# RWKV attention into a squared-ReLU FFN on one core: the opening rearranged, with weights loaded and cast by GpSimd DMAs

## The chip, the core and the metric

The kernel runs on one core of a Trainium2 chip. A core has five engines that run side by side and wait for one another through semaphores: TensorE (PE) multiplies matrices into PSUM, VectorE (DVE), ScalarE (ACT) and GpSimd (POOL) work elementwise, and SyncE (SP) issues DMAs. The metric is the time of one execution on the device, in microseconds (us). The kernel before took 206.65 us, the median of three runs from 206.44 to 207.22. The profile is of one execution, whose span from the first to the last instruction is 203.6 us.

## What is computed

The reference is a linear attention with decay, for batch 4, 8 heads, 768 positions and head size 48, and then an FFN over the 3072 tokens:

```python
def _attn_ref(r, k, v, w, u):
    state = zeros((B, H, D, D))
    for t in range(S):
        kt, vt, rt = k[:, :, t], v[:, :, t], r[:, :, t]
        cur = einsum('bhd,bhe->bhde', u[None] * kt, vt)
        y[:, :, t] = einsum('bhd,bhde->bhe', rt, state + cur)
        state = w[None, :, :, None] * state + einsum('bhd,bhe->bhde', kt, vt)
    return y
# x = y as (3072 tokens, 384)
h = maximum(x @ w_in, 0)          # w_in  384 x 2048
out = (h * h) @ w_out             # w_out 2048 x 384
```

The kernel splits the 768 positions into six chunks of 128, so there are 24 chunks (six for each of four batches), numbered so that chunks 0 to 3 are the first chunk of each batch. Inside a chunk the recurrence becomes masked matrix products, and a state per batch carries over to the next chunk. Two chunks form a group of 256 tokens; there are 12 groups.

## The kernel before

The pools, the loads and the casts. Weights arrive in float32 in sixteen slices and GpSimd casts each to bfloat16:

```python
loads = ctx.enter_context(tc.tile_pool(name="loads", bufs=7))
psA: 1 bank   psY: 1 bank   psU: 1 bank   psH: 2 banks   psO: 2 banks     # PSUM, abridged
...
def load(i):                       # r, k, v of chunk i, 192 KB each
    nc.sync.dma_start(out=rf, in_=r_v[b, c])
    nc.sync.dma_start(out=kf, in_=k_v[b, c])
    nc.sync.dma_start(out=vf, in_=v_v[b, c])
def load_w1(s):                    # load_w2 alike
    t = stage.tile([128, CCH, GT], FP32, name=f"W1f_{s}", tag="W1f", bufs=NS)
    nc.sync.dma_start(out=t, in_=w_in_t[:, :, GT * s : GT * (s + 1)])
def cast_w1(s):                    # cast_w2 alike
    t = const.tile([128, CCH, GT], BF16, name=f"W1_{s}")
    nc.gpsimd.tensor_copy(t, W1f[s])
```

The parts of a chunk: `prep` scales k and r by decays, `prep_du` and `bonus` make the term with u, `turn` transposes, `piece_A` makes the masked scores, `piece_YU` the output and the state's update, `piece_X` the transposed input of the FFN:

```python
def prep(i, eng):
    eng.tensor_mul(rk_buf[i % NB][:, 1, :, 0:D], kf, Wkhat)
    eng.tensor_mul(rk_buf[i % NB][:, 0, :, 0:D], rf, Wt2)
def prep_du(i, eng):
    eng.tensor_mul(P0, rf, kf)
    eng.tensor_mul(P0, P0, ub)
def turn(i):
    if i < 4:      # on TensorE, through a psH bank, copied out by nc.scalar.copy(rkT, pt)
    else:          # nc.sync.dma_start_transpose(rkT, src)
def piece_A(i):
    # 8 products rkT x rkT -> Ap (psA)
    for e in range(2):
        nc.vector.tensor_mul(Bm[:, e], Ap[:, e], mask_b)
def piece_YU(i):
    # products -> Y (psY) and, unless it is a batch's last chunk, U (psU)
    nc.vector.tensor_add(xs, Y, dv)
    if c < NCH - 1:
        if c == 0:
            nc.vector.tensor_mul(S0W[b], U, WLm)
        else:
            nc.vector.tensor_add(ts, U, S0W[b])
            nc.gpsimd.tensor_mul(S0W[b], ts, WLm)
def piece_X(i):
    # 3 transposes of xs -> px (psU)
    nc.scalar.copy(xTs[g][:, :, L * j : L * (j + 1)], px)
```

The FFN goes in eight pieces per group: `piece_F1` makes 256 hidden features, `piece_F2` a quarter of the output of one chunk:

```python
def piece_F1(g, s):
    hp = psH.tile([128, 2, GT], FP32, name=f"hp_{g}_{s}", tag="H")
    # 6 products W1[s] x xT -> hp
    nc.scalar.activation(hr, hp, AF.Relu)
    if s % 4 == 3:
        nc.scalar.activation(hq, hr, AF.Square)
    else:
        nc.vector.tensor_mul(hq, hp, hr)
def piece_F2(g, s):
    j, q = s // 4, s % 4               # chunk of the group, quarter of the features
    # 4 products hq x W2 -> o (psO); after q == 3: nc.scalar.copy(osb, o), DMA to out
```

The order. In a period of the steady part, step s runs FFN1 of one group, FFN2 of the group before, and attention of the group after:

```python
def att(g, s):      # a, b = 2 * g, 2 * g + 1
    s == 0: cast_v(a); piece_A(a); bonus(a)
    s == 2: cast_v(b); piece_A(b); bonus(b)
    s == 3: piece_YU(a)    s == 4: piece_YU(b)    s == 5: piece_X(a)    s == 6: piece_X(b)
def preps(g, s):    # for the next group, on GpSimd
    s == 0: prep(2g); turn(2g)          s == 2: prep_du(2g)
    s == 4: prep(2g+1); turn(2g+1)      s == 6: prep_du(2g+1)
...
for i in range(4):
    prep(i, nc.vector)
    prep_du(i, nc.gpsimd)
    turn(i)
    if i % 2 == 1:
        period(i // 2, None, None)     # attention of groups 0 and 1
for s in range(NS): cast_w1(s)
for s in range(NS): cast_w2(s)
for i in (4, 5):
    prep(i, nc.gpsimd); turn(i); prep_du(i, nc.gpsimd)
load(6); load(7)
period(None, 0, None)                  # FFN1 of group 0
period(None, 1, None)                  # FFN1 of group 1
period(2, None, 0)                     # attention of group 2, FFN2 of group 0
for g in range(2, NG + 1):
    period(g + 1 if g + 1 < NG else None, g if g < NG else None, g - 1)
```

Of the kernel before, what the change touches and what calls it, by code (L numbers as in the profile page):

```python
# [16 lines left out]
def kernel(  # L17
# [29 lines left out]
    const = ctx.enter_context(tc.tile_pool(name="const", bufs=1))  # L47
    stage = ctx.enter_context(tc.tile_pool(name="stage", bufs=3))
    loads = ctx.enter_context(tc.tile_pool(name="loads", bufs=7))
    work = ctx.enter_context(tc.tile_pool(name="work", bufs=3))  # L50
# [34 lines left out]

    W1f, W2f, W1, W2 = [], [], [], []

    def load_w1(s):
        t = stage.tile([128, CCH, GT], FP32, name=f"W1f_{s}", tag="W1f", bufs=NS)
        nc.sync.dma_start(out=t, in_=w_in_t[:, :, GT * s : GT * (s + 1)])  # L90
        W1f.append(t)

    def load_w2(s):
        t = stage.tile([128, 2, d_model], FP32, name=f"W2f_{s}", tag="W2f", bufs=NS)
        nc.sync.dma_start(out=t, in_=w_out_t[:, 2 * s : 2 * s + 2, :])
        W2f.append(t)

    def cast_w1(s):
        t = const.tile([128, CCH, GT], BF16, name=f"W1_{s}")
        nc.gpsimd.tensor_copy(t, W1f[s])  # L100
        W1.append(t)

    def cast_w2(s):
        t = const.tile([128, 2, d_model], BF16, name=f"W2_{s}")
        nc.gpsimd.tensor_copy(t, W2f[s])
        W2.append(t)
# [8 lines left out]
    for i in range(1, 4):  # L115
        load(i)
    for s in range(NS):
        load_w1(s)
    for s in range(NS):
        load_w2(s)  # L120
        if s == 3:
            load(4)
    load(5)

# [30 lines left out]
    for j in range(NB):  # L155
        t = const.tile([128, 2, H, DP], BF16, name=f"rk_{j}")
        nc.vector.memset(t[:, :, :, D:DP], 0.0)
        rk_buf.append(t)
    wrow = const.tile([1, 2, HP, 128], FP32, name="wrow")
    nc.vector.memset(wrow, 0.0)  # L160
    esel = const.tile([1, 2, 2 * D], FP32, name="esel")
    nc.vector.memset(esel, 0.0)
    nc.vector.memset(esel[:, 0, 0:D], 1.0)
    nc.vector.memset(esel[:, 1, D : 2 * D], 1.0)

# [5 lines left out]
    nc.scalar.activation(Wt2, logw, AF.Exp, scale=tcol)  # L171
    logw_p = logw.rearrange("p (a e) d -> p e a d", e=2)
    for e in range(2):
        nc.scalar.activation(  # L174
            wrow[:, e, :, 64 * e : 64 * e + D], logw_p[0:1, e], AF.Exp, scale=float(L)
        )

    WLm = const.tile([128, HP, 2 * D], FP32, name="WLm")
    wl_ps = psU.tile([128, HP, 2 * D], FP32, name="wl_ps", tag="U", padded_shape=[None, None, 128])
    for hc in range(HP):  # L180
        for e in range(2):
            nc.tensor.matmul(  # L182
                wl_ps[:, hc, :],
                wrow[:, e, hc, :],
                esel[:, e, :],
                start=(e == 0),
                stop=(e == 1),
                skip_group_check=True,
            )
    nc.scalar.copy(WLm, wl_ps)  # L190

# [33 lines left out]
    def turn(i):  # L225
        rkT = work.tile([128, 2, HP, 128], BF16, name=f"rkT_{i}", tag="rkT", bufs=4)
        rkTs[i] = rkT
        src = rk_buf[i % NB]
        if i < 4:
            pt = psH.tile([128, 2, HP, 128], BF16, name=f"pt_{i}", tag="H")  # L230
            for j in (1, 0):
                for hc in range(HP):
                    nc.tensor.transpose(
                        pt[:, j, hc, :],
                        src[:, j, 2 * hc : 2 * hc + 2, :].rearrange("p a b -> p (a b)"),
                        identity,
                    )
            nc.scalar.copy(rkT, pt)
        else:
            nc.sync.dma_start_transpose(  # L240
                rkT.rearrange("p j a t -> p (j a) t"), src.rearrange("p j h d -> p (j h d)")
            )

    def piece_A(i):
# [16 lines left out]
        Bms[i] = Bm  # L261

    def piece_YU(i):
        c, b = i // B, i % B
# [26 lines left out]
        xss[i] = xs  # L291
        if c < NCH - 1:
            if c == 0:
                nc.vector.tensor_mul(S0W[b], U, WLm)
            else:
                ts = work.tile([128, HP, 2 * D], FP32, name=f"ts_{i}", tag="ts")
                nc.vector.tensor_add(ts, U, S0W[b])
                nc.gpsimd.tensor_mul(S0W[b], ts, WLm)  # L298
# [15 lines left out]
    def piece_F1(g, s):  # L314
        xT = xTs[g]
        hp = psH.tile([128, 2, GT], FP32, name=f"hp_{g}_{s}", tag="H")
        for fi in range(2):
            for c in range(CCH):
                nc.tensor.matmul(  # L319
                    hp[:, fi, :],  # L320
                    W1[s][:, c, 128 * fi : 128 * (fi + 1)],
                    xT[:, c, :],
# [6 lines left out]
        hq = hid.tile([128, 2, GT], BF16, name=f"hq_{g}_{s}", tag=f"hq{s}")  # L329
        if s % 4 == 3:  # L330
            nc.scalar.activation(hq, hr, AF.Square)
        else:
            nc.vector.tensor_mul(hq, hp, hr)
# [4 lines left out]
    def piece_F2(g, s):  # L338
        j, q = s // 4, s % 4
        i = 2 * g + j  # L340
        if q == 0:
            ops[i] = psO.tile([128, d_model], FP32, name=f"o_{i}", tag="O", padded_shape=[None, 512])
        for f in range(4 * q, 4 * q + 4):
            nc.tensor.matmul(
                ops[i],
                hsq[g, f // 2][:, f % 2, L * j : L * (j + 1)],
                W2[f // 2][:, f % 2, :],
                start=(f == 0),
# [9 lines left out]
    def att(g, s):  # L358
        a = 2 * g
        b = a + 1  # L360
        if s == 0:
            cast_v(a)
            piece_A(a)
            bonus(a)
        elif s == 2:
            cast_v(b)
            piece_A(b)
            bonus(b)
        elif s == 3:
            piece_YU(a)  # L370
# [7 lines left out]
    def preps(g, s):  # L378
        if g >= NG:
            return  # L380
        if s == 0:
            prep(2 * g, nc.gpsimd)
            turn(2 * g)
        elif s == 2:
            prep_du(2 * g, nc.gpsimd)
        elif s == 4:
            prep(2 * g + 1, nc.gpsimd)
            turn(2 * g + 1)
        elif s == 6:
            prep_du(2 * g + 1, nc.gpsimd)  # L390

    def period(ga, g1, g2):
        for s in range(8):
            if g1 is not None:
                piece_F1(g1, s)
            if g2 is not None:
                piece_F2(g2, s)
            if ga is not None:
                att(ga, s)
                if ga > 1:  # L400
                    preps(ga + 1, s)
                if s == 7 and ga > 1:
                    load(2 * ga + 4)
                    load(2 * ga + 5)

    for i in range(4):
        prep(i, nc.vector)
        prep_du(i, nc.gpsimd)
        turn(i)
        if i % 2 == 1:  # L410
            period(i // 2, None, None)
    for s in range(NS):
        cast_w1(s)
    for s in range(NS):
        cast_w2(s)
    for i in (4, 5):
        prep(i, nc.gpsimd)
        turn(i)
        prep_du(i, nc.gpsimd)
    load(6)  # L420
    load(7)
    period(None, 0, None)
    period(None, 1, None)
    period(2, None, 0)
    for g in range(2, NG + 1):
        period(g + 1 if g + 1 < NG else None, g if g < NG else None, g - 1)

# [29 lines left out]
```

## Time and profile before

| | busy us | share of the 203.6 us span |
|---|---|---|
| TensorE (PE) | 168.7 | 83% |
| VectorE (DVE) | 133.2 | 65% |
| GpSimd (POOL) | 117.8 | 58% |
| ScalarE (ACT) | 109.9 | 54% |
| DMA queue of SyncE | 30.81 MB | 66.3% of 16 engines |

The granted clock of TensorE is 0.999 of full over the span. A line of the timeline gives the start and the duration in us, the engine, the line of the kernel, the operation, the tile written and the tiles read (buffer numbers as the program gives them), their shapes and, in brackets, how long the engine stood idle before it and what ended that. A row of the windows view gives a stretch of time, its length, the busy time of PE, of PE's weight loads, of DVE, ACT and POOL with the number of instructions, the granted clock, the busy share of the DMA engines and what they moved in GB/s.

### The profile page before, as it was taken

The page shows a single profiled execution, that of the slowest core. Times are in us where ns is not written, and L with a number is a line of the kernel's source. Part 1 is how long each engine was busy: PE and PEld are TensorE (multiplying, and loading weights), DVE is VectorE, ACT ScalarE, POOL GpSimd, SP SyncE. Part 2 cuts the span into 40 slices and gives each one's busy share as a digit, 9 for nine tenths or more (in the row PEclk, how much of TensorE's full clock was granted, in tenths as well). Part 3 has the DMA queues.
Part 4 walks back from the last instruction along what each step waited for, and adds up shares of the span by engine and source line. Part 5 has one row for each costly group of instructions (what it writes and reads, how often), then busy time and mean ns, then how long its engine had stood idle before and what let it go on. Part 6 is the DMA issues. An engine that isn't in the chain of part 4 may idle for free.

```text
span 203.6 us, 4241 instructions
## 1 busy us (share of the span) xinstructions
PE 168.7 (83%) x1624; PEld 123.2 (61%) x1624; DVE 133.2 (65%) x230; ACT 109.9 (54%) x203; POOL 117.8 (58%) x130
## 2 busy tenths in 40 slices
PE   0763647677959998998999989989989899999992
PEld 0643434455546776775767757767767577677761
DVE  4379793454966939849759489397595783963310
ACT  3360613657516484575574745755756657556640
POOL 2487973891856494692992965938929749100000
PEclk9999999999999999999999999999999999999999
DMA  5999999829714946929929649689499396311112
GB/s 109 208 209 279 384 351 252 223 52 192 146 40 94 207 118 142 197 77 194 219 54 210 152 109 214 96 176 207 60 210 180 92 210 120 84 42 39 39 40 79
DMA packets 105140, 31.07 MB, mean 153 GB/s; under 512 B 96672, under 2 KB 105120, under 8 KB 105120
## 3 DMA queue, kind: packets, MB, share of 16 engines
q1 hardware_dynamic: 105120, 30.81, 66.3%
q8 instruction: 12, 0.20, 0.4%
q14 instruction: 8, 0.07, 0.1%
HBM read 20.84 MB, written 4.72 MB: 126 GB/s over the span
## 4 chain that ended last, share of the span: by engine, by line
PE 25%; POOL 24%; DVE 20%; DMA 13%; SPq 8%; issue 5%; ACT 4%; ACTq 0%
SPq L83 2%; SPq L81 2%; DMA kf_1562<-in_k_dram 2%; DMA kf_2056<-in_k_dram 2%; DMA kf_1315<-in_k_dram 2%; DMA kf_1809<-in_k_dram 2%; DMA kf_1068<-in_k_dram 2%; DMA rf_110<-in_r_dram 2%; DMA vf_828<-in_v_dram 2%; POOL rk_180 L199 1%; POOL rk_178 L199 1%; POOL rk_182 L200 1%; POOL rk_178 L200 1%; POOL S0W_211 L298 1%; POOL rk_182 L199 1%
## 5 line engine op out<-in xcount | busy, mean ns | idle before, releaser
L319 PEld LDWEIGHTS <-W_0_439 128*128 128x128 bf16 x72 | 7.3, 102 | 3.0 <-issue 0.9
L319 PEld LDWEIGHTS <-W_2_443 128*128 128x128 bf16 x72 | 7.1, 99 | 3.3 <-issue 1.3
L182 PE MATMUL wl_ps<-esel,wrow 1*128 1x96 f32 x16 | 3.7, 423 | 6.5 <-ACT wrow L174 6.5
L319 PEld LDWEIGHTS <-W_6_451 128*128 128x128 bf16 x72 | 6.6, 97 | 2.6 <-issue 1.9
L319 PEld LDWEIGHTS <-W_3_445 128*128 128x128 bf16 x72 | 6.4, 97 | 2.9 <-issue 1.2
L319 PEld LDWEIGHTS <-W_4_447 128*128 128x128 bf16 x72 | 6.5, 97 | 2.4 <-issue 1.7
L319 PEld LDWEIGHTS <-W_1_441 128*128 128x128 bf16 x72 | 6.6, 102 | 2.0
L182 PEld LDWEIGHTS wl_ps<-esel,wrow 1*128 1x128 f32 x16 | 3.5, 325 | 6.5 <-ACT wrow L174 6.5
L319 PEld LDWEIGHTS <-W_7_453 128*128 128x128 bf16 x72 | 6.7, 98 | 0.7
L319 PEld LDWEIGHTS <-W_5_449 128*128 128x128 bf16 x72 | 6.5, 98 | 0.7
L199 POOL TENSOR_TENSOR rk_180<-kf_486,Wkhat 128x384 bf16<-128x384 f32 x1 | 1.0, 1007 | 4.9 <-DMA kf_486<-in_k_dram 4.9
L309 ACT COPY xT_315<-px_316 128x384 bf16<-128x384 bf16 x1 | 0.5, 479 | 6.2 <-PE px_316 L308 6.2
L309 ACT COPY xT_428<-px_429 128x384 bf16<-128x384 bf16 x1 | 0.5, 479 | 6.0 <-PE px_429 L308 6.0
L205 POOL TENSOR_TENSOR P_0_215<-rf_90,kf_91 128x384 f32<-128x384 f32 x1 | 1.4, 1366 | 4.0 <-DMA kf_91<-in_k_dram 4.0
L199 POOL TENSOR_TENSOR rk_176<-kf_821,Wkhat 128x384 bf16<-128x384 f32 x1 | 1.0, 998 | 4.6 <-DMA kf_821<-in_k_dram 4.6
L199 POOL TENSOR_TENSOR rk_180<-kf_1068,Wkhat 128x384 bf16<-128x384 f32 x1 | 1.0, 999 | 4.1 <-DMA kf_1068<-in_k_dram 4.1
L199 POOL TENSOR_TENSOR rk_180<-kf_1562,Wkhat 128x384 bf16<-128x384 f32 x1 | 1.0, 1007 | 4.0 <-DMA kf_1562<-in_k_dram 4.0
L199 POOL TENSOR_TENSOR rk_180<-kf_2550,Wkhat 128x384 bf16<-128x384 f32 x1 | 1.0, 1000 | 4.1 <-DMA kf_2550<-in_k_dram 4.1
L199 POOL TENSOR_TENSOR rk_180<-kf_2056,Wkhat 128x384 bf16<-128x384 f32 x1 | 1.0, 1002 | 4.0 <-DMA kf_2056<-in_k_dram 4.0
L199 POOL TENSOR_TENSOR rk_176<-kf_2303,Wkhat 128x384 bf16<-128x384 f32 x1 | 1.0, 1006 | 3.9 <-DMA kf_2303<-in_k_dram 3.9
L199 POOL TENSOR_TENSOR rk_176<-kf_1315,Wkhat 128x384 bf16<-128x384 f32 x1 | 1.0, 997 | 3.9 <-DMA kf_1315<-in_k_dram 3.9
L199 POOL TENSOR_TENSOR rk_176<-kf_1809,Wkhat 128x384 bf16<-128x384 f32 x1 | 1.0, 1004 | 3.8 <-DMA kf_1809<-in_k_dram 3.8
(1126 smaller groups left out, 669.7 us busy)
## 6 DMA issues: line engine op xcount, KB each, us to landing
W1f_116<-in_moe_w_in_dram SPq DMA_DIRECT2D x1, 384.0 KB, 4.8
W1f_118<-in_moe_w_in_dram SPq DMA_DIRECT2D x1, 384.0 KB, 5.1
W1f_120<-in_moe_w_in_dram SPq DMA_DIRECT2D x1, 384.0 KB, 5.8
W1f_122<-in_moe_w_in_dram SPq DMA_DIRECT2D x1, 384.0 KB, 6.2
W1f_124<-in_moe_w_in_dram SPq DMA_DIRECT2D x1, 384.0 KB, 6.8
W1f_126<-in_moe_w_in_dram SPq DMA_DIRECT2D x1, 384.0 KB, 6.6
W1f_128<-in_moe_w_in_dram SPq DMA_DIRECT2D x1, 384.0 KB, 6.8
W1f_130<-in_moe_w_in_dram SPq DMA_DIRECT2D x1, 384.0 KB, 6.7
```

What stands on the lines that cost most here:

```text
L81: nc.sync.dma_start(out=rf, in_=r_v[b, c])
L83: nc.sync.dma_start(out=vf, in_=v_v[b, c])
L182: nc.tensor.matmul(wl_ps[:, hc, :], wrow[:, e, hc, :], esel[:, e, :], start=(e == 0), stop=(e == 1), skip_group_check=True,)
L199: eng.tensor_mul(rk_buf[i % NB][:, 1, :, 0:D], kf, Wkhat)
L200: eng.tensor_mul(rk_buf[i % NB][:, 0, :, 0:D], rf, Wt2)
L205: eng.tensor_mul(P0, rf, kf)
L298: nc.gpsimd.tensor_mul(S0W[b], ts, WLm)
L309: nc.scalar.copy(xTs[g][:, :, L * j : L * (j + 1)], px)
L319: nc.tensor.matmul(hp[:, fi, :], W1[s][:, c, 128 * fi : 128 * (fi + 1)], xT[:, c, :], start=(c == 0), stop=(c == CCH - 1), skip_group_chec ...
```

## The change

The change rearranges the opening, up to the third FFN1 group, and some of the steady period. It is meant to let each engine work on what has arrived, so that the FFN starts before attention of group 1 is done. Its parts:

- The sixteen float32 weight loads on SyncE and the sixteen casts on GpSimd give way to eight DMAs issued by GpSimd that cast on the way, each for a quarter of a matrix.
- FFN1 of groups 0 and 1 takes its PSUM banks from psH and psO in turn, four banks instead of two.
- FFN2 of group 0 alternates between the group's two chunks, so that one quarter of W2 serves both before the next is needed.
- Chunks 2 and 3 are prepared on GpSimd. Chunk 2 is transposed by DMA, chunk 4 on TensorE; before it was the other way round.
- The first state update is a copy by ScalarE, with the multiplication on GpSimd later, instead of one multiplication on VectorE.
- WLm, the decay of a whole chunk, comes from four one-column products and four scalings instead of eight products.
- In the steady period the squares of steps 2 and 3 are on ScalarE instead of those of 3 and 7; `bonus` and `cast_v` move by a step; the odd chunk is prepared in step 1 instead of 4; one chunk is loaded in step 3 and one in step 7 instead of both in 7; `loads` has eight buffers instead of seven.

```diff
-    loads = ctx.enter_context(tc.tile_pool(name="loads", bufs=7))
+    loads = ctx.enter_context(tc.tile_pool(name="loads", bufs=8))
...
+    def load_w1(q):
+        t = const.tile([128, CCH, FQ], BF16, name=f"W1_{q}")
+        nc.gpsimd.dma_start(out=t, in_=w_in_t[:, :, FQ * q : FQ * (q + 1)])
+    def load_w2(q):
+        t = const.tile([128, 4, d_model], BF16, name=f"W2_{q}")
+        nc.gpsimd.dma_start(out=t, in_=w_out_t[:, 4 * q : 4 * q + 4, :])
...
-        if i < 4:
+        if i in (0, 1, 3, 4):
...
             if c == 0:
-                nc.vector.tensor_mul(S0W[b], U, WLm)
+                nc.scalar.copy(ts, U)
+                late.append((S0W[b], ts))
...
+        if g < 2 and s % 2 == 1:
+            hp = psO.tile([128, 2, GT], FP32, name=f"hp_{g}_{s}", tag="O")
+        else:
+            hp = psH.tile([128, 2, GT], FP32, name=f"hp_{g}_{s}", tag="H")
...
-        if s % 4 == 3:
+        if s in (2, 3) and g > 1:
             nc.scalar.activation(hq, hr, AF.Square)
...
-        j, q = s // 4, s % 4
+        j, q = (s % 2, s // 2) if g == 0 else (s // 4, s % 4)
...
+    prep(0, nc.vector); prep_du(0, nc.gpsimd); make_WLm(); turn(0)      # one call to a line in the file
+    prep(1, nc.vector); prep_du(1, nc.gpsimd); turn(1)
+    cast_v(0); piece_A(0); bonus(0)
+    prep(2, nc.gpsimd); turn(2)
+    for i in range(4, 8): load(i)
+    for q in range(4): load_w1(q)
+    cast_v(1); piece_A(1); piece_YU(0); bonus(1)
+    prep(3, nc.gpsimd); prep_du(2, nc.gpsimd)
+    piece_YU(1); piece_X(0); piece_X(1)
+    load_w2(0); load_w2(1); prep_du(3, nc.gpsimd); load_w2(2); load_w2(3)
+    turn(3); cast_v(2); piece_A(2)
+    piece_F1(0, 0); piece_F1(0, 1); bonus(2); cast_v(3); piece_A(3)
+    piece_F1(0, 2); piece_YU(2); bonus(3); piece_F1(0, 3); piece_F1(0, 4)
+    piece_YU(3); piece_F1(0, 5); piece_X(2); piece_F1(0, 6); piece_X(3); piece_F1(0, 7)
+    prep(4, nc.gpsimd); prep_du(4, nc.gpsimd)
+    for sw, ts in late[0:2]: nc.gpsimd.tensor_mul(sw, ts, WLm)
+    prep(5, nc.gpsimd); turn(5)
+    for sw, ts in late[2:4]: nc.gpsimd.tensor_mul(sw, ts, WLm)
+    prep_du(5, nc.gpsimd)
+    for s in range(8):
+        piece_F1(1, s)
+        if s == 5: turn(4)
+    # then FFN2 of group 0 in eight pieces with att(2, 0) to att(2, 6) between them
+    prep(6, nc.gpsimd); turn(6); prep(7, nc.gpsimd); turn(7)
+    prep_du(6, nc.gpsimd); prep_du(7, nc.gpsimd)
+    load(8); load(9)
...
+    for g in range(2, NG):
+        for s in range(8):
+            piece_F1(g, s)
+            F2_next()
+            if g + 1 < NG: att(g + 1, s)
+            preps(g + 2, s)
+            if s == 3: load(2 * g + 6)
+            if s == 7: load(2 * g + 7)
```

## The prediction

> **What bounds the kernel now.** I read the page first: busy time by engine, then the span in 40 slices. TensorE (PE) is the busiest engine, but its busy share is an average over stages that differ.
>
> ```profile
> PE 168.7 (83%) x1624; PEld 123.2 (61%) x1624; DVE 133.2 (65%) x230; ACT 109.9 (54%) x203; POOL 117.8 (58%) x130
> ...
> PE   0763647677959998998999989989989899999992
> ...
> DVE  4379793454966939849759489397595783963310
> ...
> DMA  5999999829714946929929649689499396311112
> ```
>
> PE's digits stay at 8 or 9 only from the thirteenth slice on, some 61 us into the run. So I cut the span at events of the timeline: the first FFN1 product (32.7), the first FFN2 product (50.7), the start of the third FFN1 group (61.2) and the end of the last FFN1 group (194.2). The windows view gives, for each stage, its length and the busy time and instruction count of each engine:
>
> ```profile
> 0.00:32.70 32.70, 15.03 (x140) 11.77 (x141) 22.22 (x42) 11.04 (x18) 21.14 (x30) 1.00 0.94 249
> 32.70:50.70 18.00, 13.16 (x99) 10.03 (x98) 7.50 (x11) 11.09 (x19) 11.04 (x12) 1.00 0.73 183
> 50.70:61.20 10.50, 8.11 (x88) 4.95 (x87) 7.97 (x13) 3.71 (x8) 6.81 (x7) 1.00 0.43 94
> 61.20:194.20 133.00, 126.87 (x1270) 93.31 (x1269) 95.50 (x164) 81.77 (x156) 78.76 (x82) 1.00 0.65 136
> ```
>
> In the last row PE is busy for 126.9 of 133.0 us: nothing there but its own work and short waits. In the first, PE is busy for 15.0 of 32.7, with VectorE (DVE) at 22.2 and DMA at 94%. **The opening is bound by DVE's chain and the transfers, the steady part by PE.** Four timeline lines show losses: a GpSimd (POOL) cast of a weight slice, which keeps POOL from other duties, the late first FFN1 product, a product in FFN1 of group 1 that waits for DVE to give a PSUM bank back, and, in the steady part, the scores of an odd chunk waiting for a DMA transpose:
>
> ```profile
> 18.53 0.82 POOL L100 CAST W_0_439<-W1f_116 128x768 bf16<-128x768 f32 x1 [0.97 <-DMA W1f_116<-in_moe_w_in_dram]
> ...
> 32.76 1.49 PE L319 MATMUL hp_0_497<-xT_315,W_0_439 128*128 128x256 bf16 x6
> ...
> 45.05 0.81 PE L319 MATMUL hp_2_607<-xT_428,W_2_443 128*128 128x256 bf16 x6 [0.75 <-DVE hq_0_594 L333]
> ...
> 121.20 0.40 PE L251 MATMUL Ap_1890<-rkT_1744 48*128 48x128 bf16 x8 [0.84 <-DMA rkT_1744<-rk_182]
> ```
>
> [...] No GpSimd DMA is in this trace[...]. [...] chunk loads 4 and 5, queued beside weights, took 5.6 to 8.6 us to land against 3.2 to 4.9 for chunks 6 and 7. [...] the writes of rk_182 took 1.17 us on DVE beside POOL casts, the second write of rk_180, same shapes, 0.55.
>
> **The change part by part, in trace time.**
>
> 1. *Casts off POOL.* Sixteen casts of about 0.87 us, 13.9 us, go. Eight DMA issues come. I have no trace of one on POOL; SyncE's eight W1f issues took 0.49 to 1.15 us, mean 0.73 (5.87 over 8), and the new tiles are twice as large. My estimate is 1.2 us of POOL each, 9.6 in sum. This is the number I trust least. POOL also takes preps 2 and 3 from DVE (four multiplies of about 1.0) and the four first state multiplies (1.0 each, L298), so its opening does not get shorter; its order changes.
>
> 2. *First FFN1 product.* POOL finishes the bonus inputs of chunks 0 and 1 at about 12.8 as now (11.59 plus 1.19). Then prep 2 to 14.8, four W1 issues to 19.6, prep 3 to 21.6. Transposes of chunk 3 on PE follow to 22.3, then the scores of chunk 2, then FFN1 from **22.8** instead of 32.76. Chunks 0 and 1 don't hold that up: DVE drops the four preps of chunks 2 and 3 and the state products, and xT of group 0 should be there near 19.5. The first W1 tile, issued by 16, lands by about 21: 768 KB at the 378 GB/s that 20 to 25 us shows is 2.1 us, about doubled for the chunk loads beside it, plus latency.
>
> 3. *FFN1 of groups 0 and 1.* Now 18.0 us for 16 pieces: with two banks a piece costs about 1.1, as relu (0.60 on ACT), square (0.69 on DVE) and product form a loop. Four banks break it, but chunks 2 and 3 move in here, and DVE becomes the limit. Its work for group 0: masks 2 x 1.28, bonus 2 x 1.10, xs 2 x 0.55, eight squares x 0.69 = 5.5; 11.4 us in all, from 22.9, plus about 1.2 of waits[...]: 35.5. Group 1: eight squares, 5.5 us: **41.0**, with PE done at 40.3. W1 quarters are needed at 22.8, 26.5, 32 and 34, which leaves room.
>
> 4. *FFN2 of group 0 with attention of group 2.* DVE again: 2 x (1.28 + 1.10 + 0.55 + 0.55) = 7.0 us from 41.3 is 48.3; then transposes and xT copies (0.48 each) to 50. FFN1 of group 2 starts at **50.0** instead of 61.26. Weaving the two chunks over the quarters of W2 lets PE run under DVE. The last W2 quarter is asked for at about 47. All transfers from 15.5 on need 6.29 MB / 378 GB/s = 16.6 us for weights plus twelve chunk loads of 0.945 us each (196.6 KB at 208 GB/s) = 11.3: done at 43.5 if casting costs the engines nothing. **Gain to here 11.2 us.**
>
> 5. *A new wait.* On POOL prep 6 stands behind the state multiplies of chunks 4 and 5, the last of which waits for ts of chunk 5 at 48.2. Now prep 6 ran at 51.7, before them. So: state 49.2, prep 6 to 51.2, its DMA transpose about 2.8 us later (121.20 less 118.41): 54.0. Scores of chunk 6 are due at 51.3 (50.0 plus 1.3). PE stands for **2.7 us, a loss**.
>
> 6. *Steady part.* Starts of FFN1 run from 61.26 to 183.93, nine periods of 13.63 on average; one I took apart is 13.89 long, of which 0.9 is the transpose wait and 0.1 a wait for xs, so 12.9 without stalls. Preparing the odd chunk in step 1 instead of 4 removes the transpose wait (seven of them, 0.5 to 0.9). One square moved to ACT and the bonus put after hq_1 shorten DVE's chain to xs by about 0.7, just enough for it not to become the next wait; I leave 0.2. Nine periods of 13.1 are 117.9 against 122.7: **gain 4.8**. Tail unchanged: 9.4 after the last FFN1, in both.
>
> Also smaller: the float32 matmuls for WLm (3.72 us of PE now, eight products against four of one column after), which delayed the first transposes from about 8 to 10.1; this only helps the chain of item 2, where POOL's order and the landing of chunk 1 count, so I add nothing for it.
>
> Sum: 11.2 - 2.7 + 4.8 = 13.3. From 206.65, about **193.4 us**.
>
> **Rivals.**
> (a) [...] At 2.5 us an issue, POOL is 10.4 us later by prep 5 and the bonus of chunk 5, FFN1 starts near 28, group 2 near 56.5: total near 199. [...] Against: SyncE's issues are short.
> (b) *The casting transfer is slow.* At half rate weights need 33 us, the last quarter lands past 55, and FFN2 of group 0 waits 8 to 10 us: near 202. Nothing in this trace speaks for or against; only the sums of bytes speak.
> (c) *The steady gain is hidden.* DVE's chain (6.7 us from hq_0 to xs) takes the transpose's place at the single Y bank. In the period from 170.68, without a transpose wait, PE still waited 0.45 for hq_1 and 0.2 for xs, and it took 13.25. Then only 2 us come: near 196.
> (d) *POOL barely notices the issues.* Then all of items 2 to 4 moves up by 2 to 4 us, to where the first W1 tile is the limit: near 190.
>
> **Range and chances.** (a), (b) and (c) push up and can add; (d) pushes down. I take 193.4, with 188.0 to 200.5 as the range for 8 in 10. Within 2% begins at 202.5, which needs (a) or (b) in full and more: 0.08. Slower by 2% would need transfers at a quarter of the rate seen: 0.03. Faster by over 2%: 0.89.
>
> **What would show it.** In the profile after: eight DMA issues on POOL near 1.2 us each; no casts; first FFN1 product near 22.8 and third group near 50; DVE busy over 90% from 23 to 41; one PE wait of 2 to 3 us for the transpose of chunk 6; periods near 13.1 and no wait on transposes later. If FFN1 starts after 27, look at POOL's issues (a). If FFN1 or FFN2 waits for W tiles, (b). If periods stay at 13.4 or more with waits for xs or ts, (c). The prediction is wrong if the opening is paced by something I did not place: chunk loads starved by weight packets on the shared DMA engines would show as POOL waiting for kf of chunk 4 or 5.

## The result and the profile after

The changed kernel takes **198.38 us** (median of four runs, 197.27 to 200.87) against 206.55 us for the kernel before, measured with it: ratio 0.9588, 95% interval 0.9502 to 0.9675. Ratios here leave out executions in the slower state that some show, in this one that of 200.87. The change is faster by about 8 us where 13.3 were predicted. The profiled execution spans 195.5 us against 203.6.

The page of the changed kernel, cut to the lines that answer to those of before, with the slices of TensorE's granted clock (tenths of full speed) added:

```profile
PE 164.1 (84%) x1616; PEld 119.9 (61%) x1616; DVE 132.3 (68%) x222; ACT 111.5 (57%) x206; POOL 121.2 (62%) x135
...
PE   0535968941956999799999999999999999999992
...
PEclk9999999995799999999999999999999999999999
DMA  5999999998028879599486875986759761011112
```

PE reaches 9 in the fifth slice, where before it did so in the eleventh. But there is a hole that the kernel before didn't have: PE's ninth and tenth slices stand at 4 and 1, the granted clock is at 5 and 7 in the tenth and eleventh, and DMA falls to 0 in the eleventh (a slice is 4.9 us). Something stopped the work at some 42 to 48 us.

The windows view of the changed kernel, cut at the same events as before (first FFN1 product, first FFN2 product, third FFN1 group, end of the last FFN1 group):

```profile
0.00:21.90 21.90, 9.09 (x86) 6.90 (x86) 11.02 (x20) 9.97 (x19) 16.21 (x29) 1.00 0.93 174
21.90:38.90 17.00, 14.12 (x144) 11.46 (x143) 14.48 (x24) 12.50 (x23) 10.08 (x13) 1.00 1.25 190
38.90:56.10 17.20, 9.51 (x88) 5.45 (x86) 8.33 (x14) 3.48 (x8) 9.85 (x10) 0.80 0.56 116
56.10:186.10 130.00, 125.35 (x1267) 92.67 (x1267) 97.53 (x163) 83.48 (x154) 85.04 (x86) 1.00 0.64 141
```

The lengths tell the whole story against before: 32.7 to 21.9 us (10.8 gained), 18.0 to 17.0 (1.0 gained, though chunks 2 and 3 are now in it), **10.5 to 17.2 (6.7 lost)**, 133.0 to 130.0 (3.0 gained); the tail has 9.4 in both. Sum 8.1, as the spans say. In the third row no engine is busy for more than 9.9 of 17.2 us, at a clock of 0.80.

The timeline of the changed kernel shows the hole. First the POOL rows, then PE's:

```profile
14.44 3.24 POOL L90 DMA_DIRECT2D W<-in_moe_w_in_dram  x4
...
21.95 1.55 POOL L95 DMA_DIRECT2D W<-in_moe_w_out_dram  x2
...
25.54 1.55 POOL L95 DMA_DIRECT2D W<-in_moe_w_out_dram  x2
33.84 1.00 POOL L183 TENSOR_TENSOR rk<-kf,Wkhat 128x384 bf16<-128x384 f32 x1 [6.76 <-DMA kf<-in_k_dram]
...
40.73 1.00 POOL L183 TENSOR_TENSOR rk<-kf,Wkhat 128x384 bf16<-128x384 f32 x1 [0.99 <-DMA kf<-in_k_dram]
...
40.48 1.46 PE L334 MATMUL o<-W,hq 128*128 128x384 bf16 x8 [0.43 <-DVE hq L323]
48.29 0.61 PE L235 MATMUL Ap<-rkT 48*128 48x128 bf16 x8 [6.35 <-DMA rkT<-rk]
48.83 2.68 PE L334 MATMUL o<-W,hq 128*128 128x384 bf16 x8
...
56.11 0.81 PE L309 MATMUL hp<-xT,W 128*128 128x256 bf16 x6 [0.70 <-ACT xT L296]
...
59.92 0.40 PE L235 MATMUL Ap<-rkT 48*128 48x128 bf16 x8 [2.35 <-DMA rkT<-rk]
```

Eight weight issues take 3.24 + 1.55 + 1.55 = 6.3 us, 0.8 each. The casts are gone. Then POOL stands 6.76 us for kf of chunk 4 (33.84) and prepares chunk 5 at 40.73; TensorE stands 6.35 us for that chunk's transpose (48.29), and the next eight FFN2 products take 2.68 us where eight of the same shape took 1.46 at 40.48: the granted clock was 0.50 from 44.5 to 51.3. The third group starts at 56.11. The last line is the wait for chunk 6 that the prediction had named.

The chain of the changed kernel between 30 and 49 us, followed back from what ended last (start, length, what):

```profile
29.81 10.79 DMA kf<-in_k_dram
...
44.58 3.67 DMA rkT<-rk
...
48.29 0.61 PE Ap L235 x6
```

A load of 192 KB took 10.79 us from issue to landing, and kf of chunk 4, asked for at 16.53, took 17.2; the median of the kf loads in this run is 3.7. About half of the 10.79 passed in the issue itself. SyncE's own rows (SPq) in the timeline:

```profile
17.21 7.53 SPq L82 DMA_DIRECT2D vf<-in_v_dram  x1
24.78 4.98 SPq L80 DMA_DIRECT2D rf<-in_r_dram  x1
29.81 5.17 SPq L81 DMA_DIRECT2D kf<-in_k_dram  x1
```

An issue usually takes about 0.7 us (median of the 24 kf loads 0.69). Here each stood while the loads before it had not landed. What held the loads up is shown by the DMA view of the changed kernel for 24 to 36 us, by queue (packets, MB, share of 16 engines); q0 is GpSimd's queue with the weights, q1 SyncE's with the chunks:

```profile
q0 software_dynamic: 2247, 1.79, 93.1%
q1 hardware_dynamic: 2247, 0.43, 32.3%
```

**2247 packets each: one for one.** A packet of the weights is 768 or 1024 bytes as written, one of a chunk load 192 bytes. So in these 12 us the chunk loads got 0.43 MB, 36 GB/s, while the weights had 149. In shorter stretches it is the same: 386 and 386 packets from 30 to 32 us, 399 and 400 from 32 to 34. With packets of such different size, equal numbers starve the queue with the small ones.

### The profile page after: what moved, and what is told of

Read it like the earlier page. It is cut to its first block, busy times and chain, and to the rows that moved or that the text cites. A ratio compares the mean times of both kernels' runs of the same rounds, so it can differ in the third digit from the quotient of the medians.

```text
span 195.5 us, 4203 instructions
## 1 busy us (share of the span) xinstructions
PE 164.1 (84%) x1616; PEld 119.9 (61%) x1616; DVE 132.3 (68%) x222; ACT 111.5 (57%) x206; POOL 121.2 (62%) x135
## 4 chain that ended last, share of the span: by engine, by line
PE 48%; DVE 16%; DMA 14%; SPq 10%; POOL 7%; ACT 2%; issue 1%; POOLq 0%
PE o L334 22%; PE hp L309 19%; DMA kf<-in_k_dram 8%; DVE Bm L244 5%; SPq L82 5%; DMA rkT<-rk 4%; DVE dv L206 4%; SPq L80 3%; DVE hq L323 3%; DVE du L201 2%; POOL rk L183 2%; DMA rf<-in_r_dram 2%; POOL rk L184 2%; PE Y L255 2%; PE px L295 2%; PE Ap L235 2%
## 5 line engine op out<-in xcount | busy, mean ns | idle before, releaser
L318 ACT ACTIVATE hr<-hp 128x512 bf16<-128x512 f32 x96 | 57.3, 597 | 44.2 <-PE hp L309 43.3
L309 PE MATMUL hp<-xT,W 128*128 128x256 bf16 x576 | 78.4, 275 | 1.0 <-ACT xT L296 0.7
L334 PE MATMUL o<-W,hq 128*128 128x384 bf16 x384 | 77.7, 330 | 0.4 <-DVE hq L323 0.4
L323 DVE TENSOR_TENSOR hq<-hp,hr 128x512 bf16<-128x512 f32 x76 | 51.9, 688 | 34.4 <-ACT hr L318 34.3
L309 PEld LDWEIGHTS <-W 128*128 128x128 bf16 x576 | 53.2, 99 | 11.8 <-issue 1.5
L334 PEld LDWEIGHTS <-hq 128*128 128x128 bf16 x384 | 37.7, 99 | 16.9 <-issue 1.6
L244 DVE TENSOR_TENSOR Bm<-Ap,maskJT 128x512 bf16<-128x512 f32 x48 | 30.8, 682 | 11.9 <-PE Ap L235 11.9
L189 POOL TENSOR_TENSOR P<-rf,kf 128x384 f32<-128x384 f32 x24 | 25.0, 1040 | 3.8 <-DMA kf<-in_k_dram 3.8
L190 POOL TENSOR_TENSOR P<-P,ub 128x384 f32<-128x384 f32 x24 | 24.1, 1005 | 2.6 <-DMA ub<-in_u_dram 0.8
L184 POOL TENSOR_TENSOR rk<-rf,Wt 128x384 bf16<-128x384 f32 x22 | 24.0, 1089 | 0.0
L235 PE MATMUL Ap<-rkT 48*128 48x128 bf16 x192 | 10.4, 233 | 10.8 <-DMA rkT<-rk 9.3
L276 DVE TENSOR_TENSOR xs<-Y,dv 128x384 bf16<-128x384 f32 x24 | 13.1, 547 | 0.9 <-PE Y L260 0.8
```

What stands on the lines that cost most here:

```text
L235: nc.tensor.matmul(Ap[:, e, hc, :], rkT[p0 : p0 + D, 1, hc, :], rkT[p0 : p0 + D, 0, hc, :], start=True, stop=True, skip_group_check=True,)
L309: nc.tensor.matmul(hp[:, fi, :], W1[s // 2][:, c, GT * (s % 2) + 128 * fi : GT * (s % 2) + 128 * (fi + 1)], xT[:, c, :], start=(c == 0), s ...
L334: nc.tensor.matmul(ops[i], hsq[g, f // 2][:, f % 2, L * j : L * (j + 1)], W2[q][:, f % 4, :], start=(f == 0), stop=(f == FCH - 1), skip_gr ...
```

## The experiments

Theory S: the chunk loads are starved by the weight packets, and this alone keeps the third group from 50. Its rivals are that the transpose's own latency, the order on POOL, or the half clock is the cause. The steady part and the banks have tests of their own.

**Weights left out.** The W tiles are set to zero by GpSimd and nothing is loaded into them; everything else stays. The FFN's output is zero, so the time is that of a kernel with no weight transfer.

```diff
-        nc.gpsimd.dma_start(out=t, in_=w_in_t[:, :, FQ * q : FQ * (q + 1)])
+        nc.gpsimd.memset(t, 0.0)
-        nc.gpsimd.dma_start(out=t, in_=w_out_t[:, 4 * q : 4 * q + 4, :])
+        nc.gpsimd.memset(t, 0.0)
```

> Leaves out the eight weight transfers: the weight tiles are set to zero by GpSimd instead, all else as in the changed kernel. Theory A (chunk loads starved by the weight packets, one small packet let through for each large one): without the weights chunk 5 lands by about 27 us, GpSimd does not wait 6.8 us for k of chunk 4, the 6.35 us wait of TensorE for the transpose of chunk 5 falls below 1 us, the half-clock stretch after it goes, and the third FFN1 group starts at 47 to 49 us instead of 56.1; time 189 to 192 us. Theory B (the order of SyncE's queue alone: the transpose of chunk 5 stands behind the loads of chunks 6 and 7): at most 2 us less, 196 us. Theory C (GpSimd has too much to do before chunk 5): 3 us less at most, as the issues themselves took 4.8 us.

Measured: 193.05 us, ratio 0.9373 (0.9332 to 0.9413). From the timeline of this run:

```profile
14.72 5.33 POOL L90 MEMSET W<- 128x1536 bf16 x4
...
19.13 0.94 SPq L81 DMA_DIRECT2D kf<-in_k_dram  x1
...
31.25 1.01 POOL L183 TENSOR_TENSOR rk<-kf,Wkhat 128x384 bf16<-128x384 f32 x1
...
37.43 1.00 POOL L183 TENSOR_TENSOR rk<-kf,Wkhat 128x384 bf16<-128x384 f32 x1
...
44.42 0.40 PE L235 MATMUL Ap<-rkT 48*128 48x128 bf16 x8
```

No bracket stands behind the three last lines: POOL doesn't wait for kf any more and TensorE doesn't wait for chunk 5. kf of chunks 4 to 7 landed 3.4 to 4.4 us after the issue, and no issue of these loads took more than 1.75 us. The third group starts at 51.58, later than expected: the zeroing costs POOL 1.33 us a tile where an issue costs 0.8, prep 4 is at 31.25 for that reason and not for a load, and FFN2 begins at 41.46 instead of 38.91. From there to the third group it is 10.1 us instead of 17.2. The wait of 2.35 for chunk 6 stays, and against the expectation a slow stretch comes after it, at about 56 to 59 us: six FFN1 products take 1.46 us at 55.72 and 0.83 at 60.39. Without weight traffic the hole is gone.

**Chunk 5 transposed on TensorE.** This takes the transpose out of SyncE's queue and the DMA engines, and leaves the loads as they are.

```diff
-        if i in (0, 1, 3, 4):
+        if i in (0, 1, 3, 4, 5):
...
-    turn(5)
...
     att(2, 1)
     F2_next()
+    turn(5)
```

> Only the transpose of chunk 5 moves from DMA to TensorE, between two chunk products of FFN2 of group 0. Both theories: GpSimd's write of its source ends at 42.7 us, then 0.6 us on TensorE and 1.0 us of copy, so the scores of chunk 5 start near 44.4 instead of 48.3 us: 3.9 us less, and 1 us more if the half-clock stretch gets shorter; 192 to 194 us. What is left of the wait (about 2.5 us) is the share of the late chunk load (A).

Measured: 194.01 us, 0.9448 (0.9395 to 0.9502). kf of chunk 4 is as late as before (33.89, after a wait of 6.63), but the scores of chunk 5 come at 44.40 and the third group at 52.41. Doing this transpose by DMA cost 3.9 us of the hole (48.29 less 44.40): its stand in SyncE's queue from 42.7 to 44.6 and the transfer of 3.67, less the copy that TensorE's way needs (1.01). The half clock still came (0.50 from 45 to 47 us), though the longest wait here was 1.10 us: the eight FFN2 products after it took 2.74 us.

**Loads 6 and 7 behind the transpose of chunk 5 in SyncE's queue.**

```diff
-    for i in range(4, 8): load(i)
+    for i in range(4, 6): load(i)
...
     prep(5, nc.gpsimd); turn(5)
+    load(6); load(7)
```

> Only the loads of chunks 6 and 7 move behind the transpose of chunk 5 in SyncE's queue. Theory B: the transpose is issued at once when GpSimd has written its source (42.7 instead of 44.6 us) and has the DMA engines to itself, so TensorE's wait falls from 6.35 to 3 or 4 us, but the loads of 6 and 7 come later by as much; 195 to 198 us. Theory A: k of chunk 5 still lands near 40.7 us, so most of the wait stays.

Measured: 195.64 us, 0.9498 (0.9447 to 0.9548). kf of chunk 4 at 34.06, prep 5 at 41.13, both as in the changed kernel. But the transpose is issued at once (43.11), the wait for chunk 5 is 3.17 us instead of 6.35, the eight products after it take 1.47 us at a granted clock of 1.00, and the third group starts at 52.79. Part of the shorter wait is only that TensorE came 0.8 us later. From the written source to the scores of chunk 5 it is 2.8 us (43.1 to 45.9) instead of 5.6 (42.7 to 48.3): about half of that was a transpose behind loads, and beside loads, that nobody needed yet.

**Chunks 6 and 7 prepared before the state products of group 2.** This tests the wait of 2.35 us that step 5 of the prediction named.

```diff
     att(2, 1)
+    prep(6, nc.gpsimd); turn(6); prep(7, nc.gpsimd); turn(7)
     F2_next()
...
-    prep(6, nc.gpsimd); turn(6); prep(7, nc.gpsimd); turn(7)
```

> Only GpSimd's order changes: chunks 6 and 7 are prepared before the state products of chunks 4 and 5. If the wait of 2.35 us for the transpose of chunk 6 comes from that order (step 5 of the prediction), it goes and so does the 0.4 us for chunk 7: 194.5 to 195.5 us. If something else holds that transpose (the landing of chunk 6, the transfers), it stays and the time is 197 to 198 us.

Measured: 195.18 us, 0.9494 (0.9451 to 0.9537). The wait for chunk 5 stays at 6.07 and the third group starts at 57.32, 1.2 us later, but the scores of chunk 6 follow at 58.72 without a wait. The cause that step 5 gave, POOL's order, is shown.

**W2 asked for later, and chunk 5 on TensorE.** The four W2 issues stand behind the preparation of chunk 4. The edit of the run with chunk 5 on TensorE is in it too.

```diff
-    load_w2(0); load_w2(1); prep_du(3, nc.gpsimd); load_w2(2); load_w2(3)
+    prep_du(3, nc.gpsimd)
...
-    prep(4, nc.gpsimd); prep_du(4, nc.gpsimd)
+    prep(4, nc.gpsimd); load_w2(0); load_w2(1)
+    prep_du(4, nc.gpsimd); load_w2(2); load_w2(3)
```

> As the run with chunk 5 transposed on TensorE, and the four W2 transfers are issued after chunk 4 has been prepared instead of before, so nothing but W1 stands beside the loads of chunks 4 and 5. Theory A (small packets let through one for one beside weight packets): k of chunk 4 lands soon after W1 is through (26 us), GpSimd prepares chunk 4 at 27 to 28 instead of 33.9 us and chunk 5 by 38 instead of 42.7, TensorE finds chunk 5 transposed when it comes to it, no idle stretch, no half clock; third FFN1 group at 48.5 to 49.5 us against 52.4, time 189.5 to 191. If the chunk loads are slow for another reason, chunk 4 stays near 33 us and the time near 193.5; if W2 now comes too late for FFN2 of group 0, TensorE waits there for W2 tiles and the time is 193 or more.

Measured: 192.53 us, 0.9273 (0.9208 to 0.9337). Faster, but the expected times were missed: kf of chunk 4 was there at 30.4 (13.3 us after its issue), the third group started at 51.49. No W2 moves by then. W1, which moves until about 27.5 us, and chunk 2's transpose ahead of these loads are enough to hold chunk 4 back. With chunks 6 and 7 prepared earlier as well:

> The same with chunks 6 and 7 prepared before the state products of chunks 4 and 5. The waits are at different places, so the gains should add: another 2.7 us less than the run before it, 187 to 188.5 us. If the loads of chunks 6 and 7, now beside W2, land too late (after 47 us), a wait for the transpose of chunk 6 stays and the gain is under 1 us.

Measured: **191.15 us, 0.9196 (0.9119 to 0.9273)**. kf of chunk 4 comes at 31.36 after a wait of 6.92; third group 51.98, chunk 6 without a wait. That is 1.4 us less than the run before it, half of what was expected, and by the intervals not clearly a gain: the wait for chunk 6 goes, but the third group starts 0.5 us later.

**Chunk 2 on TensorE, added to that version.** In it the DMA engines moved only 20 to 90 GB/s from 16.8 to 19.6 us (the expectation below says 17 to 21.5, but from 20 to 22 they moved 164 to 214), while the DMA transpose of chunk 2 was under way. The change had moved that transpose from TensorE to SyncE's queue, ahead of chunk loads 4 to 7. This run puts it back on TensorE.

```diff
-        if i in (0, 1, 3, 4, 5):
+        if i in (0, 1, 2, 3, 4, 5):
...
-    turn(2)
...
     piece_A(1); piece_YU(0)
+    turn(2)
```

> The version of run c1_all with chunk 2 transposed on TensorE as well (its DMA transpose and its wait in SyncE's queue go). In c1_all the DMA engines moved only 20 to 70 GB/s from about 17 to 21.5 us, while that transpose ran, and kf of chunk 4 was there at 31.36. Theory S (the transpose takes transfer time from everything queued behind it): about 4 us x 130 GB/s = 0.5 MB more are moved by 22 us, so kf of chunk 4 lands 1.5 to 2.5 us earlier (29 to 30), third group at 50 to 51, 189 to 190.5 us. Rival (packet for packet beside the weights is all that counts, the weights just finish earlier): kf of chunk 4 within 0.5 us of 31.36, third group near 52, 191 us as c1_all.

Measured: **190.48 us, 0.9261 (0.9219 to 0.9303)**. The POOL rows for chunks 4 and 5, and PE's for the scores of chunk 5, in the timeline of this run:

```profile
23.98 0.99 POOL L183 TENSOR_TENSOR rk<-kf,Wkhat 128x384 bf16<-128x384 f32 x1
...
32.92 0.99 POOL L183 TENSOR_TENSOR rk<-kf,Wkhat 128x384 bf16<-128x384 f32 x1
...
44.42 0.40 PE L235 MATMUL Ap<-rkT 48*128 48x128 bf16 x8 [1.10 <-ACT rkT L222]
```

Both chunks are prepared without a wait, chunk 4 more than 7 us earlier and not the 1.5 to 2.5 expected. kf of chunk 4 was asked for at 14.10 instead of 16.93, before the first weight packets moved, and landed 5.7 us later. Yet the third group starts only 0.7 us earlier, at 51.29: preparation is off the path now. What is left is the order of FFN2 and DVE, with 1.1 us of waiting for ScalarE's copy of the transpose of chunk 5. By their intervals this run and the last can't be told apart, so the total decides between neither theory; the times of kf do. Both beat the changed kernel.

**The same alone: the changed kernel with only chunk 2 back on TensorE.** W2 is asked for early here.

> The changed kernel with one part of the change undone: chunk 2 is transposed on TensorE again, as in the kernel before, in place of the DMA transpose that the change put ahead of chunk loads 4 to 7 in SyncE's queue. Theory T (that transpose starts the starvation: it holds back the loads of chunk 4 until the weight packets are there to alternate with; from run c2): POOL finds kf of chunk 4 without a wait, prepares it near 23 to 25 instead of 33.84, and only chunk 5 still has to share with the weights: prep 5 at 34 to 38, its DMA transpose about 4 us later, wait for it 0 to 3 us instead of 6.35, third group at 51 to 53 instead of 56.11, then the wait of 2.4 for chunk 6: 191.5 to 195 us. Theory W (the weight packets alone starve the loads of chunks 4 and 5, wherever the transpose runs, and c2 gained from its late W2): kf of chunk 4 still missing at 30 or later, wait for chunk 5 of 5 us or more, third group at 55 to 56, 196.5 to 199 us.

Measured: 196.35 us, 0.9532 (0.9495 to 0.957), between the two ranges. Theory T holds for chunk 4, theory W for chunk 5 and the third group. From the timeline of this run:

```profile
27.82 1.01 POOL L183 TENSOR_TENSOR rk<-kf,Wkhat 128x384 bf16<-128x384 f32 x1
...
39.19 1.00 POOL L183 TENSOR_TENSOR rk<-kf,Wkhat 128x384 bf16<-128x384 f32 x1 [5.24 <-DMA kf<-in_k_dram]
...
47.16 0.61 PE L235 MATMUL Ap<-rkT 48*128 48x128 bf16 x8 [4.16 <-DMA rkT<-rk]
```

Chunk 4 is no longer missing (POOL prepares it at 27.82 because it issues W2 until then), but kf of chunk 5, asked for at 18.48, lands at 39.05, 20.6 us later; in the DMA view of 24 to 36 us the packets stand at 2195 for the weights to 2191 for the chunks. The third group starts at 55.13. One repair alone moves the starvation to the next chunk.

**Two banks instead of four for FFN1 of groups 0 and 1.**

```diff
-        if g < 2 and s % 2 == 1:
+        if False:
```

> The changed kernel with two PSUM banks instead of four for the FFN1 pieces of groups 0 and 1; all else as changed. Theory S (step 3 of the prediction: four banks break the loop of relu, square and product, which takes 1.1 us a piece on two banks; but with chunks 2 and 3 woven in, DVE's 16.9 us of work set the end anyhow, and in the run of the changed kernel the next group then stood still for the starved chunk 5): FFN1 of groups 0 and 1 gets 1 to 3 us longer (end at 40 to 42 instead of 38.9), the wait of 6.35 us for the transpose of chunk 5 shrinks by as much, and the third group starts at 56 to 57; 197 to 199 us in all, that is 0 to +1 us on the changed kernel. Rival (the banks carry the opening): FFN1 of groups 0 and 1 takes 18 us or more again plus the woven chunks, third group at 60 or later, 201 to 204 us.

Measured: 198.11 us, 0.9643 (0.9569 to 0.9717), no difference from the changed kernel that can be told. FFN1 of group 1 ends at 43.7 instead of 39.1 (42.22 and 37.60, each plus 1.47), more than expected, with 5.3 us of waits for squares to give a bank back; but the wait for chunk 5 shrinks from 6.35 to 3.19 and the third group starts at 57.00. The four banks are worth 4.6 us to their stage, and the hole behind it swallows nearly all of it.

**The kernel before with only the weight DMAs of the change.** Eight issues stand where the sixteen casts were, the sixteen SyncE loads go; order, banks and preparation stay.

```diff
-    for s in range(NS): cast_w1(s)
-    for s in range(NS): cast_w2(s)
+    for q in range(4): load_w1(q)
+    for q in range(4): load_w2(q)
...
```

> The kernel before with one thing of the change: eight casting GpSimd DMAs in place of the sixteen SyncE loads with sixteen casts, at the place of the casts; order, banks and preparation stay as before. Theory S (the opening of the kernel before is bound by DVE's chain and by the order of the products, POOL's casts were beside it): POOL's work falls by 13.9 less 6.4 = 7.5 us, but the first FFN1 product stays at 31 to 33 and the third group at 60 to 62, since the weight packets now stand beside the chunk loads 4 and 5 as much; 204 to 207 us, ratio 0.985 to 1.00. Rival (the casts on POOL were what held the opening): first FFN1 product at 25 to 28, third group at 54 to 57, 199 to 202 us.

Measured: 205.14 us (20 runs), 0.9967 (0.9944 to 0.999). The first FFN1 product starts at 32.82 (32.76 before) and the third group at 60.52 (61.26). POOL does 110.0 us of work instead of 117.8. That freed time was not on the path: taking the casts off POOL by itself brings 0.3%. What gains the 10.8 us of the first stage is the rest of the change: the new order, with chunks 2 and 3 prepared on POOL and the state products off DVE. Which of these gains how much was not tested.

**The steady preparation put back** (odd chunk prepared in step 4, both loads in step 7, du in steps 2 and 6).

```diff
-        elif s == 1:
+        elif s == 4:
             prep(2 * g + 1, nc.gpsimd)
             turn(2 * g + 1)
...
```

> The changed kernel with the steady preparation as it was: odd chunk prepared in step 4, bonus inputs in steps 2 and 6, both loads in step 7. Theory S1 (the transpose wait of the odd chunk cost its full 0.5 to 0.9 us a period): seven or more such waits return, periods rise from 12.9 to 13.5, 4 to 5 us more than the changed kernel, 202 to 203 us. Theory S2 (VectorE's chain hides it): 1 to 2 us more, 199.5 to 200.5.

Measured: 202.63 us, 0.9763 (0.9705 to 0.9822). PE's waits between 62 and 186 us, of this run:

```profile
PE Ap L235 <- DMA rkT<-rk: 7.3, 7, 1.4
```

and of the changed kernel:

```profile
PE Y L255 <- DVE xs L276: 1.8, 3, 1.2
PE Ap L235 <- DMA rkT<-rk: 0.4, 1, 0.4
```

Seven waits for the odd chunk's transpose are back, 0.50 to 1.45 us each. From the scores of chunk 6 to those of the last even chunk, eight periods, it is 109.3 us instead of 105.3.

**Squares, bonus and casts put back into their old steps** (ScalarE squares 3 and 7; bonus with the scores).

```diff
-        if s in (2, 3) and g > 1:
+        if s % 4 == 3 and g > 1:
...
```

> The changed kernel with squares on ScalarE in steps 3 and 7 again and the bonus and the cast back in their old steps, from group 3 on; the preparation stays early. If VectorE's chain to xs is what limits the period once the transpose wait is gone, it is longer by one square (0.69 us), TensorE waits for xs or hq_1 in most periods, and periods rise from 12.9 to 13.3 or 13.5: 202 to 203 us. If PE's own work limits it, 198 to 199 us.

Measured: 204.41 us, 0.9848 (0.9797 to 0.9899). PE's waits in the same stretch of this run:

```profile
PE hp L309 <- DVE hq L323: 5.3, 9, 1.3
PE Ap L235 <- DMA rkT<-rk: 2.3, 1, 2.3
```

The one wait for a transpose is that of chunk 6, which falls into the stretch here; later transposes are in time. The eight periods take 110.8 us, 5.5 more than in the changed kernel. So each half of the steady change is needed: without the early preparation TensorE waits for the transpose, without the moved squares it waits for DVE.

All runs side by side. The chips differ, and with them the kernel before (205.58 to 207.22 us), so the ratios compare better than the times. The intervals of four versions (loads 6 and 7 moved; chunks 6 and 7 earlier; chunk 2 alone on TensorE; two banks) overlap with that of the changed kernel: what these show is in their timelines, not in their totals. The three versions with late W2 can't be told apart by their totals either.

| version | us | ratio to before | third group at |
|---|---|---|---|
| before | 206.55 | 1 | 61.26 |
| changed | 198.38 | 0.9588 | 56.11 |
| weights left out | 193.05 | 0.9373 | 51.58 |
| chunk 5 on TensorE | 194.01 | 0.9448 | 52.41 |
| loads 6, 7 behind transpose 5 | 195.64 | 0.9498 | 52.79 |
| chunks 6, 7 prepared earlier | 195.18 | 0.9494 | 57.32 |
| late W2, chunk 5 on TensorE | 192.53 | 0.9273 | 51.49 |
| the same, chunks 6, 7 earlier | 191.15 | 0.9196 | 51.98 |
| the same, chunk 2 on TensorE | 190.48 | 0.9261 | 51.29 |
| changed, chunk 2 on TensorE | 196.35 | 0.9532 | 55.13 |
| changed, two banks | 198.11 | 0.9643 | 57.00 |
| before, weight DMAs alone | 205.14 | 0.9967 | 60.52 |
| changed, old preparation | 202.63 | 0.9763 | 56.90 |
| changed, old squares | 204.41 | 0.9848 | 58.02 |

## Why the prediction was right, and where it was wrong

The direction was right and 198.38 us lies in the range, in its upper part. The excess of 5 us over 193.4 comes from step 4.

1. *Issues on POOL*: 0.8 us each, not 1.2. Rival (a), 2.5 us an issue, is out; nor did the cheaper issues bring rival (d)'s 190. That casting didn't make the transfer dear here (against rival (b)) I read from the packets: one of W1, 2048 bytes read and 1024 written, held an engine for 95 ns from 18 to 24 us (950 packets in 94.0% of 16 engines' time), or 47 ns a KB read; in the kernel before one of 1024 bytes without a cast took 45 ns from 20 to 24 us and 53 from 17 to 20.
2. *First FFN1 product*: 21.9 against 22.8. The number is right, the path was another, so part of it is luck. POOL was through with prep 3 at 20.0 and not 21.6, but TensorE came to the transposes of chunk 3 only at 20.14, after it had waited for xs of chunk 1 on DVE until 19.85; xT of group 0, expected near 19.5, was there at 20.9. The run with the weight DMAs alone shows that taking away the casts is not enough.
3. *FFN1 of groups 0 and 1*: PE done at 39.1 against 40.3. Right, and the run with two banks shows the loop of bank, relu and square that step 3 named. DVE was busy for 15.4 of the 18 us from 23 to 41, 86% and not over 90%. The first products were slow in both kernels: six took 1.28 us in the kernel before against 0.65 later, twelve took 2.48 us in the changed kernel at 21.92 and 1.47 at 25.70. The granted clock was 1.00 there; what made them slow is not shown.
4. *Third group*: 56.11 against 50.0. **This step failed.** It added up bytes: all transfers were to be done at 43.5, so chunk 5 would be in time. The engines did move nearly that much, 5.2 MB as written from 15.5 to 43.5 us of some 5.5 for the weights and the twelve loads, but the sum doesn't say who is served. The weight quarters were served ahead of need, and chunks 4 and 5 got one packet of 192 bytes for each of 768 or 1024. At the 36 GB/s measured, the 0.59 MB of the three tiles of chunk 5 take 16 us by estimate. The sentence at the end of the prediction named just this symptom, but no number of the sum was made from it. The part of the change that step 4 passed over is chunk 2's DMA transpose: with it back on TensorE, chunk 4 is no longer missing. Starvation alone, as theory S had it, is not the whole cause. Three things add up in the hole: the starvation of chunks 4 and 5, the transpose of chunk 5 behind later loads, and the half clock, which alone cost 1.2 us on the first eight products (2.68 less 1.46). In the best version the third group starts at 51.3, so 1.3 us of the 6.1 stay. There DVE stands 1.26 us for the scores of chunk 5, behind ScalarE's copy of the transpose, which step 4 did not have; the changed kernel transposes chunk 5 by DMA, so the runs don't say what is left of its own order.
5. *Wait for chunk 6*: 2.35 and 0.40 us against 2.7. Right, with its cause shown.
6. *Steady part*: the nine periods take 120.2 us; 117.9 plus the wait of 2.7 were predicted. The sum is right, in part by luck: the first two periods take 15.7 and 14.2 us, with 2.75 us of waits for the transposes of chunks 6 and 7 and 1.18 for xs, and the last seven have a mean of 12.90 us, less than the 13.1 predicted. Rival (c) is out for this kernel, but the run with the old squares shows that it would have been right without them: DVE's chain does take the transpose's place then, and costs more than I gave it.

One example of the prediction is not clean: the second write of rk_180 (20.70, 0.55 us), set there against the writes of rk_182 beside POOL casts, also overlapped a POOL cast (20.74), which took 1.19 us instead of 0.82. So there POOL was the slow one.

What stays open: how chunk 2's transpose and the weights hold each other up. Without weights this transpose landed 2.8 us after its issue and kf of chunk 4 3.4 us after its own; in the changed kernel it was 6.8 and 17.2. In the run with late W2 and chunks 6 and 7 earlier, a weight packet held an engine for 153 ns on average from 14 to 22 us, while the transpose ran (480 packets in 57.3% of 16 engines' time), instead of some 95. But when the weights set in, the rate also falls without this transpose: to 90 GB/s from 17 to 18 us in the run with only chunk 2 back on TensorE, with the engines 67% busy. Whether chunk 4 is held back by the packets of the transpose or by the later issue of the loads behind it, the runs don't separate.

## What to carry to other kernels

Before moving a big transfer to a second queue, ask for each small transfer that is in flight with it what it gets if the packets of both go through in equal numbers, as they did here (2247 of each in 12 us): its packet size over the sum of both, not its share of the bytes (here 192 bytes beside some 800 got 36 of 185 GB/s, a fifth). Issue the big transfer late, in parts as they are needed (late W2: ratio 0.9273 against 0.9448), and the small urgent one first; don't put something urgent behind loads for later (TensorE stood 3.17 us for the transpose of chunk 5 ahead of loads 6 and 7, 6.35 behind them). A repair upstream is worth only what the next late arrival leaves of it (with chunk 2 alone back on TensorE, chunk 4 was prepared 6.0 us earlier and the third group came 1.0 us earlier), so look at the wait after next before counting a gain.

## What the hardware showed that I had not expected

- Writing zeros to a tile of 128 x 1536 bf16 takes GpSimd 1.33 us, more than issuing a casting DMA that fills it (0.8 us).
- SyncE itself can stand in an issue: one of a chunk load took 7.53 us at 17.21 in the changed kernel, where 0.7 is usual (median of the 24 vf loads 0.74), and none more than 1.75 in the same stretch without weights. What holds it is not shown.
- In these runs the length of one wait doesn't tell whether TensorE's clock falls. In the changed kernel it fell to 0.50 at about 44.5 us, after 2.5 us without a product, and came back at about 51.3, 3.0 us after the products had set in again. In the run with chunk 5 on TensorE it was 0.72 from 44 to 45 us and 0.50 from 45 to 47 with no wait over 1.10 us; in the run with loads 6 and 7 moved 3.17 us of idling left it at 1.00. After a wait of 2.34 to 2.37 us for chunk 6 four FFN2 products took 1.34 us in that run and 1.49 in the one without weights, but 0.81 in the changed kernel and with late W2. What makes it fall in one run and not in another stays open.
